# A hand-planned attention block on one core: the planner's transfer queue, the last output tile of block 2, and the first key evacuation

## The chip, the core and the metric

The kernel runs on one core of one Trainium2 chip. The metric is device microseconds (us) of one execution. Before the change the median of three runs is 410.35 us (410.2 to 410.64). Names used below: PE is TensorE (matmul), ACT is ScalarE, DVE is VectorE, POOL is GpSimd, SP is SyncE, which here only issues transfers (DMAs).

## The reference, cut to what matters

```python
# x (1, 2048, 448), wqkv (448, 1344), wo (448, 448), all bf16; 16 heads of 28
qkv = (x @ wqkv).reshape(B, S, 3, H, Dh).transpose(2, 0, 3, 1, 4)
q, k, v = qkv[0], qkv[1], qkv[2]
scores = einsum("bhqd,bhkd->bhqk", q, k) * Dh ** -0.5
p = softmax(scores, axis=-1)
o = einsum("bhqk,bhkd->bhqd", p, v)
out = o.transpose(0, 2, 1, 3).reshape(B, S, D) @ wo
```

## The kernel before, in words

**Tiles.** The 16 heads are four groups (g) of four heads, each head padded from 28 to 32 rows; the 2048 queries are four blocks (c) of 512. A window is one group and one query block; there are 16. In a window, every key tile of 128 keys (16 of them) gives four score tiles, one for each head, of 128 keys by 512 queries: 1024 score tiles in all. A score tile is one matmul (line 854) of a key tile (KB) and a query tile (QB). Both hold 64 rows for a head: 32 of the head and 32 that carry a bound on the scores, so that the exponent never overflows; the bound's rows are filled by transfers (KB<-NK at lines 591 and 613, QB<-QP at line 706).

**Exponentials on two routes.** Most score tiles go in pairs through ACT: two matmuls fill the two banks of PA0 or PA1, one activation (line 1277) of 128x1024 writes PTA. The others go through one bank of PD and a polynomial: three DVE passes (lines 1058, 1061, 1077) and one POOL product (line 1064), or one DVE copy (line 990) and six POOL passes (lines 997 to 1020). They write PTD. The value product (line 1122) then takes the four exponentials of a key tile into PO; a column of ones in VA sums the denominators.

**The planner.** The order of every engine's instructions is not written down. The function builds a list of `Op`s with an estimated duration, a latency, dependencies and a priority, runs a small event loop over them (lines 1313 to 1375) with one clock for PE, ACT, POOL, DVE and SP, and then issues the instructions in the order of the planned start times (lines 1380 to 1392). At run time each engine takes its own instructions strictly in that order and waits on semaphores where data is missing. Which route a score tile takes is also decided there, by which buffer is free at the planned time. So a changed constant can move any instruction behind it.

**Normalizing a window.** When a window's last value product is done, DVE copies PO to OSB (line 942). SP fetches the sums (line 949), DVE inverts them (line 951), SP stores them to DRAM (line 952) and reads them back as a broadcast over 128 partitions, 256 KB (line 954, RRB), for which the planner counts a latency of GLAT = 6.5. POOL multiplies (line 957) and leaves OT for the output projection. The same SP queue carries the query transfers of the next windows: two copies (line 700) and four bound rows (line 706), each planned with QLAT = 2.6.

**Key bounds.** For groups 1 to 3, `task_kmax` makes the largest key per row (line 571), then NK on DVE (line 615), then four broadcast transfers (line 613). For group 0 the first 512 keys do not go over transfers: their score columns in PD0 are evacuated by ACT, twice, to KB0_0 and KB0_1 (line 538).

**Start.** The input is loaded, transposed on PE (line 414), evacuated (lines 425, 427), projected to keys (line 522) and queries (line 652); DVE writes the bound rows of the first two query tiles itself (line 678).

**End.** In the last group, `task_OP` makes the output of a query block from its four OT tiles, four 128-row tiles (tq) for each block: matmuls at line 804, then a DVE evacuation. For blocks 2 and 3 the first three groups were summed earlier (`SPLIT`, `task_part`), so that only the last group is missing and DVE adds the two (line 808). One transfer stores a block (line 817). The last block is done by hand behind the plan (lines 1393 to 1408): DVE transposes PO (line 866), inverts the sums (867), transposes them back in halves (870), multiplies (1399); PE projects (1401); ACT or DVE evacuates (1407, 1405); four transfers store (1408). The first three groups' share for tiles 0, 1 and 3 is put into PD banks by nine matmuls (line 888, `late_sums`).

Of the kernel before, what the change touches and what calls it, by code (L numbers as in the profile page):

```python
# [9 lines left out]
ACT = mybir.ActivationFunctionType  # L10
ALU = mybir.AluOpType
# [7 lines left out]
P = 128  # L19
H = 16  # L20
HP = 32
G = 4
HG = 4
CC = 4
QW = 512
# [57 lines left out]
def kernel(  # L83
# [7 lines left out]
    nc = tc.nc  # L91
    _, S, D = x.shape
    Dh = D // H
    CK = D // CC
    NQC = S // QW
    NKT = S // P
    TPC = QW // P
# [41 lines left out]
    QEA = 20  # L139
    PLT = 6.0  # L140
    GLAT = 6.5
    J3 = 9
    UQ = 60
    OD = 2
# [6 lines left out]
    LOOK = 0.2  # L151
    SLK = 0.13
    MG = 0.1
    SPLIT = {2: (0, 1, 2, 3), 3: (2,)}
    ACCQ = (0, 1, 3)
    ACCP = 2000
    PARTD = 60
# [19 lines left out]
    KP0 = -4395  # L177
    KP1 = -4000
    VE = 16
    UV = 4  # L180
    BW = (-1, 2, 0)
    THF = (0, 1, 0, 0)
    EVP = (-1200, -4365, -700, 0)
    KEVP = (0, 200, 200, 200)
# [134 lines left out]
    log = []  # L319
# [9 lines left out]
    def add(op):  # L329
        static[op.eng].append(op)  # L330
        return op

    def bank_task():
        return {"slot": None}
# [173 lines left out]
    def task_K(g, sc):  # L508
# [19 lines left out]
        if g == 0:  # L528
# [8 lines left out]
            if sc == 0:  # L537
                evs = [add(Op("ACT", 0.67, lambda pr=pr: nc.scalar.activation(
                    out=KB[0][pr][:, cs], in_=ap(), func=ACT.Identity, bias=bndcol[pr][:, 0:1], scale=selcol[pr][:, 0:1]),
                    deps=[ops[-1], redmm], prio=KP0 if pr == 0 else KP1, lat=0.17)) if pr == 0 or KENG[0] == "ACT" else  # L540
                    add(Op("DVE", EVK, lambda pr=pr: nc.vector.tensor_scalar(
                        out=KB[0][pr][:, cs], in0=ap(), scalar1=selcol[pr][:, 0:1], scalar2=bndcol[pr][:, 0:1], op0=ALU.mult, op1=ALU.add),
                        deps=[ops[-1]], prio=-4360)) for pr in range(2)]
                for i in range(HG):
                    kev[(g, sc, i)] = evs[i // 2]
            else:
                evs = [add(Op("ACT", 0.62, lambda: nc.scalar.activation(
                    out=KB[1][0][:, cs], in_=ap(), func=ACT.Identity, bias=onescol[:, 0:1], scale=1.0),
                    deps=[ops[-1]], prio=prio + KEVP[sc], lat=0.17) if KENG[sc] == "ACT" else Op("DVE", EVK, lambda: nc.vector.tensor_scalar(  # L549
                        out=KB[1][0][:, cs], in0=ap(), scalar1=onescol[:, 0:1], scalar2=None, op0=ALU.add),  # L550
                        deps=[ops[-1]], prio=prio + 0.1 + KEVP[sc]))]
                k0ev[sc] = evs[0]
                evs[0].acq = lambda t: red.start is None or red.done(t)
                red.acq = lambda t: evs[0].start is None or evs[0].done(t)
# [12 lines left out]
    def task_kmax(g):  # L567
# [42 lines left out]
        def rep_out(i, c0):  # L610
# [1 line left out]
            n = (S - c0 * QW) // P  # L612
            nc.sync.dma_start(out=KB[g % 2][i // 2][HP * st:HP * (st + 1), c0 * QW:S].rearrange("p (r q) -> p r q", q=P),
                              in_=NK[g][HP * SI[i]:HP * (SI[i] + 1), None, :].to_broadcast([HP, n, P]))
        nk = add(Op("DVE", 0.2, lambda: nc.vector.tensor_scalar(
            out=NK[g][:], in0=maskm[:, 0:P], scalar1=KMAX[g][:, 0:1], scalar2=None, op0=ALU.mult), deps=[m], prio=prio + 0.2, elig=elig))
        for i in (2, 3, 0, 1):
            o = add(Op("SP", DISS + 0.07, (lambda i=i: rep_out(i, c0)), deps=[nk] + ([deps[i]] if i < 2 else []),
                       prio=due + 0.3 + 0.001 * i, lat=DLAT + 0.6))
# [176 lines left out]
    def task_OP(c):  # L796
        due = (12 + c + 1) * WT + 16
        st = add(Op("SP", 0.05, None, prio=due))
        evs = []
        for tq in range(TPC):  # L800
            task = bank_task()
            ap = (lambda task=task: bank(task)[:, 0:D])
            g0 = G - 1 if c in SPLIT else 0
# [9 lines left out]
            def aft(t, task=task):  # L813
                task["slot"].free_at = t + SEM
            ev.after = aft
            evs.append(ev)
        add(Op("SP", 0.05, lambda: nc.sync.dma_start(out=out_perm[:, c * TPC:(c + 1) * TPC, :], in_=OUTS[c][:]),
               deps=evs, prio=due))

    SEGS = [(FB * w, FB * (w + 1)) for w in range(NF)] + [(FB * NF + (NKT - FB) * w, FB * NF + (NKT - FB) * (w + 1)) for w in range(NF)]  # L820

# [494 lines left out]
    times = [0.0]  # L1316
    port = [0.0]
    lock = [0.0]
    seen = set()
    ends = []  # L1320
    seq = 0
    while True:
# [12 lines left out]
        while progress:  # L1335
            progress = False
            for e in ("ACT", "PE", "POOL", "DVE", "SP"):
# [27 lines left out]
                    heapq.heappush(times, t + o.dur + PGAP)  # L1365
                o.start = t
                o.end = t + o.dur
                free[e] = o.end
                log.append((t, seq, o))
                seq += 1  # L1370
# [9 lines left out]
    log.sort(key=lambda e: (e[0], e[1]))  # L1380
    sync = mybir.DependencyInfo(mybir.DependencyClass.Sync, mybir.DependencyReason.DATA)
    issued = []
    for _, _, o in log:
        if o.fn is None:
            continue
        r = o.fn()
        if o.eng == "DVE" and r is not None:
            issued.append((o, r))
        elif o.eng == "POOL" and o.kind in ("p", "n", "g"):
            before = [d for d in issued[-8:] if d[0].end <= o.start + 1e-6 and (d[0].kind == "sb" or d[0].end <= o.start - PLD + 1e-6)]  # L1390
            if before:
                tc.add_manual_dep(r.ins, before[-1][1].ins.name, sync)
    c = NQC - 1
    g = G - 1
    hw = QW // 2
    fb = {tq: PD[late_acc[tq]][:, 0:D] if tq in late_acc else PA[1 - acts[-1][2].idx][:, 0:D] for tq in range(TPC)}

    def half_out(hf):
        nc.vector.tensor_tensor(out=OTL[hf], in0=PO[:, hf * hw:(hf + 1) * hw], in1=DEN[hf], op=ALU.mult)
        for tq in (2 * hf, 2 * hf + 1):  # L1400
            nc.tensor.matmul(out=fb[tq], lhsT=OTL[hf][:, (tq % 2) * P:(tq % 2 + 1) * P], rhs=WO[:, g, :], start=(tq not in late_acc), stop=True)
    norm_dve(PO[:], DT[:], DR[:], lambda hf: DEN[hf], half_out)
    for tq in range(TPC):
        if tq in SPLIT[c]:
# [31 lines left out]
```

## Time and profile before

| what | us |
|---|---|
| median of three runs | 410.35 |
| span of the profiled execution, first to last instruction | 408.4 |
| median less that span | 1.95 |
| ACT busy, share of the span | 394.3 (97%) |
| DVE busy | 382.0 (94%) |
| PE busy | 359.9 (88%) |
| POOL busy | 329.2 (81%) |
| last exponential ends (timeline of ACT) | 399.2 |

The profiled execution has no other time of its own than its span; the 1.95 us are what the runs' median has beyond it. The profile has a page (shares, a strip of 40 slices, the costliest groups) and answers questions of the trace: a timeline of one engine, the chain of work that ended last, who waited for whom. A timeline row gives the start, the length, the engine, the line, the operation, the tiles, the shape and how many equal instructions were merged in it; in brackets stands the idle time ahead of it and what ended that. Two ACT instructions that follow each other overlap in it: the next one starts before the last has written all of its output, so the distance between ends is what an exponential costs.

### The profile page before, as it was taken

What the parts mean: (1) busy time and instruction counts of PE and PEld (TensorE: products, weight loads), DVE (VectorE), ACT (ScalarE), POOL (GpSimd) and SP (SyncE); (2) the same over time, 40 slices, a digit from 0 to 9 for tenths busy, and PEclk for the clock granted to TensorE, in tenths of its full rate; (3) what the DMA queues carried; (4) which work ended last, traced back from release to release, by engine and by line L of the source; (5) the groups of instructions that cost most, each with busy time, mean ns of one, the idle gap of its engine ahead of it and who ended that gap; (6) DMA issues with size and microseconds to landing.
All of it is one profiled execution on the core that took longest, in us unless ns stands there. A gap on an engine that the chain in (4) does not pass through costs nothing.

```text
span 408.4 us, 7572 instructions
## 1 busy us (share of the span) xinstructions
PE 359.9 (88%) x2599; PEld 120.2 (29%) x2599; DVE 382.0 (94%) x673; ACT 394.3 (97%) x433; POOL 329.2 (81%) x352
## 2 busy tenths in 40 slices
PE   8999989798898989889898989888898988889994
PEld 5243232223233232322323232232322222223231
DVE  6996999999999999999999999999999999999985
ACT  4999999999999999999999999999999999999992
POOL 4048999778699889978697987999679988999870
PEclk9999999999999999999999999999999999999998
DMA  9251130101501020110501000010230001010112
GB/s 220 44 86 43 42 76 2 29 30 39 108 1 34 13 40 0 24 52 6 104 2 46 2 20 29 8 41 2 64 80 3 28 4 43 2 35 13 49 72 90
DMA packets 36302, 16.58 MB, mean 41 GB/s; under 512 B 28768, under 2 KB 32992, under 8 KB 36264
## 3 DMA queue, kind: packets, MB, share of 16 engines
q1 hardware_dynamic: 35656, 15.89, 16.5%
q8 instruction: 20, 0.33, 0.3%
q10 hardware_dynamic: 608, 0.22, 0.2%
q14 instruction: 18, 0.15, 0.1%
HBM read 7.44 MB, written 1.97 MB: 23 GB/s over the span
## 4 chain that ended last, share of the span: by engine, by line
ACT 55%; PE 25%; DVE 11%; issue 7%; DMA 1%; DVEq 0%; ACTq 0%
ACT PTA L1277 54%; PE PA L854 9%; PE PO L1122 7%; PE PD L854 3%; DVE DU L1058 2%; DVE DV L1061 2%; DVE PTD L1077 1%; DMA QB<-QP 1%; PE PO L652 1%; PE PA L393 1%; DVE QB L678 1%; PE PO L1238 1%; DVE QB L662 1%; DVE KB L549 1%; DVE KB L557 1%
## 5 line engine op out<-in xcount | busy, mean ns | idle before, releaser
L1277 ACT ACTIVATE PTA<-PA 128x1024 bf16<-128x1024 f32 x422 | 387.3, 1183 | 0.4 <-PE PA L854 0.2
L1064 POOL TENSOR_TENSOR DG<-DV,DU 128x512 f16<-128x512 f16 x157 | 179.9, 1156 | 49.5 <-DVE DV L1061 40.4
L854 PE MATMUL PA<-QB,KB 64*128 64x512 bf16 x843 | 168.3, 380 | 38.3 <-ACT PTA L1277 35.6
L854 PEld LDWEIGHTS <-KB 64*128 64x128 bf16 x1024 | 66.2, 93 | 180.7 <-issue 173.4
L1058 DVE TENSOR_SCALAR DU<-PD 128x512 f16<-128x512 uint16 x157 | 104.3, 680 | 7.2 <-PE PD L854 6.7
L1077 DVE SCALAR_TENSOR_TENSOR PTD<-PD,DG 128x512 uint16<-128x512 f32 x157 | 105.6, 680 | 3.1 <-POOL DG L1064 2.2
L1061 DVE SCALAR_TENSOR_TENSOR DV<-PD,DU 128x512 f16<-128x512 uint16 x157 | 104.5, 678 | 0.6
L1122 PE MATMUL PO<-PTA,VA 128*32 128x512 bf16 x843 | 86.4, 386 | 0.6 <-DVE QB L662 0.4
L854 PE MATMUL PD<-QB,KB 64*128 64x512 bf16 x181 | 65.6, 377 | 1.8 <-DVE PTD L1077 0.9
L1122 PE MATMUL PO<-PTD,VA 128*32 128x512 bf16 x181 | 52.9, 386 | 0.0
L1122 PEld LDWEIGHTS <-VA 128*32 128x32 bf16 x1024 | 19.7, 94 | 50.4 <-issue 49.7
L1003 POOL TENSOR_TENSOR GV<-GE,GU 128x512 f16<-128x512 f32 x24 | 27.8, 1159 | 2.5 <-DVE QP L691 0.8
L1005 POOL TENSOR_TENSOR GU<-GV,GU 128x512 f16<-128x512 f16 x24 | 27.8, 1156 | 1.5 <-DVE QP L691 0.8
L1007 POOL TENSOR_TENSOR SG<-SG,GU 128x512 f32<-128x512 f32 x24 | 27.8, 1157 | 1.2 <-DVE QP L691 0.6
L997 POOL TENSOR_SCALAR GU<-SG 128x512 f16<-128x512 uint16 x24 | 14.9, 619 | 7.5 <-DVE SG L990 4.7
L990 DVE COPY SG<-PD 128x512 f32<-128x512 f32 x24 | 16.4, 681 | 4.0 <-PE PD L854 3.8
L957 POOL TENSOR_TENSOR OT<-OSB,RRB 128x512 bf16<-128x512 f32 x15 | 19.1, 1273 | 0.4 <-DVE QP L691 0.4
L652 PE MATMUL PO<-XT,WQP 112*128 112x512 bf16 x56 | 18.7, 386 | 0.4 <-DVE KB L549 0.4
L1020 POOL TENSOR_SCALAR PTD<-SG 128x512 uint16<-128x512 f32 x24 | 14.9, 620 | 3.0 <-DVE QP L691 1.9
L1000 POOL TENSOR_SCALAR GE<-SG 128x512 f32<-128x512 uint16 x24 | 14.9, 619 | 1.9
L723 PEld LDWEIGHTS <-XT 112*128 112x128 bf16 x256 | 13.4, 98 | 9.4 <-issue 9.2
L522 PE MATMUL PO<-XT,WKP 112*128 112x512 bf16 x48 | 15.9, 386 | 0.0
(105 smaller groups left out, 194.2 us busy)
## 6 DMA issues: line engine op xcount, KB each, us to landing
RRB<-SCR SPq DMA_DIRECT2D x15, 256.0 KB
QB<-QP SPq DMA_DIRECT2D x56, 32.0 KB
KB<-NK SPq DMA_DIRECT2D x12, 128.0 KB
XS<-in_x_dram SPq DMA_DIRECT2D x3, 448.0 KB
out_dram<-XS SPq DMA_DIRECT2D x3, 448.0 KB
QB<-QB SPq DMA_DIRECT2D x28, 32.0 KB
KB<-KB SPq DMA_DIRECT2D x6, 128.0 KB
RRB<-SCRF SPq DMA_DIRECT2D x2, 256.0 KB
```

Of the source, the lines that this page charges most:

```text
L652: ops = chain_mm(CC, lambda cc: nc.tensor.matmul(out=ap(), lhsT=WQP[g][:, cc, :], rhs=XT[c][cc // 2][0:CK, cc % 2, :], start=(cc == 0), st ...
L854: nc.tensor.matmul(out=ap, lhsT=KB[g % 2][i // 2][a:a + 64, j * P:(j + 1) * P], rhs=QB[w % NQB][i // 2][a:a + 64, :], start=True, stop=Tru ...
L957: o5 = add(Op("POOL", 1.22, lambda: nc.gpsimd.tensor_tensor(out=OT[g][c][:], in0=OSB[b][:], in1=RRB[b][:], op=ALU.mult), deps=o4, prio=-10 ...
L1003: g3 = add(Op("POOL", PTT, lambda: nc.gpsimd.tensor_tensor(out=GV[:], in0=GE[:], in1=GU[:], op=ALU.mult), deps=[g2], prio=prio + 2, kind=" ...
L1005: g4 = add(Op("POOL", PTT, lambda: nc.gpsimd.tensor_tensor(out=GU[:], in0=GV[:], in1=GU[:], op=ALU.mult), deps=[g3], prio=prio + 3, kind=" ...
L1007: g5 = add(Op("POOL", PST, lambda: nc.gpsimd.tensor_tensor(out=X[:], in0=X[:], in1=GU[:], op=ALU.add), deps=[g4], prio=prio + 4, kind="g", ...
L1058: p1 = add(Op("DVE", P1, lambda: nc.vector.tensor_scalar(out=DU[b][:], in0=lo, scalar1=SIG / 65536, scalar2=SIG * (SS - 0.5), op0=ALU.mult ...
L1061: p2 = add(Op("DVE", P1, lambda: nc.vector.scalar_tensor_tensor(out=DV[b][:], in0=lo, scalar=65536 * (SS - 0.5 + CE / C3), in1=DU[b][:], o ...
L1064: gq = add(Op("POOL", PTT, lambda: nc.gpsimd.tensor_tensor(out=DG[b][:], in0=DV[b][:], in1=DU[b][:], op=ALU.mult), deps=[p2], prio=n, kind ...
L1077: f = add(Op("DVE", P1, lambda: nc.vector.scalar_tensor_tensor(out=PTD[st["s"].idx][:].bitcast(U16), in0=PX[slot.idx][:], scalar=EBITS + C ...
L1122: nc.tensor.matmul(out=PO[HP * st:HP * (st + 1), :], lhsT=VA[g][:, j, st, :], rhs=r["p"][i][1](), start=first, stop=last, tile_position=(0 ...
L1277: nc.scalar.activation(out=PTA[pslot.idx][:, 0:len(ns) * QW], in_=PA[s.idx][:, 0:len(ns) * QW], func=ACT.Exp, bias=ACT_BIAS, scale=ACT_SCALE)
```

## The change

It has four parts, all in the one function.

1. **Planner.** When SP issues a broadcast with latency GLAT, the planner notes the time until which the queue is taken (RNGB = 6.2 behind the issue). A transfer that SP issues before that time is planned to land not before it, each 0.35 (RNGN) behind the last. This alters planned latencies, so the order of instructions; it adds no instruction.
2. **Last output tile of block 2.** Tile 3 of block 2 leaves `SPLIT` and `task_OP`. `late_tile` makes it right behind the last value product in the issue order: four matmuls (all four groups) into the free half of a PA buffer, a copy on ACT, a transfer of 112 KB of its own. The other three tiles are stored by one transfer of 336 KB. The three `late_sums` matmuls of tile 3 of block 3 are held back and issued behind the first half of the last projection.
3. **First key evacuation.** KB0_0 of group 0's first 512 keys is evacuated by DVE (`tensor_scalar`) and no longer by ACT; KB0_1 stays on ACT and is planned behind it.
4. **Smaller ones.** NK of groups 1 to 3 moves from DVE to POOL; BW, which tells after which of the first window's four bound rows a transposed input is evacuated, goes from 2 to 4 for input block 1.

```diff
+    RNGB = 6.2
+    RNGN = 0.35
...
-    SPLIT = {2: (0, 1, 2, 3), 3: (2,)}
+    SPLIT = {2: (0, 1, 2), 3: (2,)}
+    ATQ = 3
...
-    BW = (-1, 2, 0)
+    BW = (-1, 4, 0)
...
                 evs = [add(Op("ACT", 0.67, lambda pr=pr: nc.scalar.activation(
                     out=KB[0][pr][:, cs], in_=ap(), func=ACT.Identity, bias=bndcol[pr][:, 0:1], scale=selcol[pr][:, 0:1]),
-                    deps=[ops[-1], redmm], prio=KP0 if pr == 0 else KP1, lat=0.17)) if pr == 0 or KENG[0] == "ACT" else
+                    deps=[ops[-1], redmm], prio=KP1, lat=0.17)) if pr else
                     add(Op("DVE", EVK, lambda pr=pr: nc.vector.tensor_scalar(
                         out=KB[0][pr][:, cs], in0=ap(), scalar1=selcol[pr][:, 0:1], scalar2=bndcol[pr][:, 0:1], op0=ALU.mult, op1=ALU.add),
-                        deps=[ops[-1]], prio=-4360)) for pr in range(2)]
+                        deps=[ops[-1], redmm], prio=KP0)) for pr in range(2)]
+                evs[1].deps.append(evs[0])
...
-        nk = add(Op("DVE", 0.2, lambda: nc.vector.tensor_scalar(
-            out=NK[g][:], in0=maskm[:, 0:P], scalar1=KMAX[g][:, 0:1], scalar2=None, op0=ALU.mult), deps=[m], prio=prio + 0.2, elig=elig))
+        nk = add(Op("POOL", 0.25, lambda: nc.gpsimd.tensor_scalar(
+            out=NK[g][:], in0=maskm[:, 0:P], scalar1=KMAX[g][:, 0:1], scalar2=0.0, op0=ALU.mult, op1=ALU.add), deps=[m], prio=prio + 0.2, elig=elig))
...
         for tq in range(TPC):
+            if c == NQC - 2 and tq == ATQ:
+                continue
...
-        add(Op("SP", 0.05, lambda: nc.sync.dma_start(out=out_perm[:, c * TPC:(c + 1) * TPC, :], in_=OUTS[c][:]),
+        n = len(evs)
+        add(Op("SP", 0.05, lambda: nc.sync.dma_start(out=out_perm[:, c * TPC:c * TPC + n, :], in_=OUTS[c][:, 0:n, :]),
                deps=evs, prio=due))
+
+    def late_tile(ap):
+        c, tq = NQC - 2, ATQ
+        for g in range(G):
+            nc.tensor.matmul(out=ap, lhsT=OT[g][c][:, tq * P:(tq + 1) * P], rhs=WO[:, g, :], start=(g == 0), stop=(g == G - 1))
+        nc.scalar.copy(out=OUTS[c][:, tq, :], in_=ap)
+        nc.sync.dma_start(out=out_perm[:, c * TPC + tq:c * TPC + tq + 1, :], in_=OUTS[c][:, tq:tq + 1, :])
...
+    ring = [0.0]
...
+                if e == "SP" and o.fn is not None and pos[0] > 0:
+                    if o.lat == GLAT:
+                        ring[0] = t + RNGB
+                    elif t < ring[0]:
+                        ring[0] += RNGN
+                        o.lat = max(o.lat, ring[0] - o.end)
...
+    last_v = [o for _, _, o in log if o.kind == "V"][-1]
+    spare = PA[1 - acts[-1][2].idx]
+    held = []
     for _, _, o in log:
         if o.fn is None:
             continue
+        if o.kind == "A" and o.prio >= ACCP + ACCQ[-1]:
+            held.append(o)
+            continue
         r = o.fn()
+        if o is last_v:
+            late_tile(spare[:, QW:QW + D])
...
         for tq in (2 * hf, 2 * hf + 1):
             nc.tensor.matmul(out=fb[tq], lhsT=OTL[hf][:, (tq % 2) * P:(tq % 2 + 1) * P], rhs=WO[:, g, :], start=(tq not in late_acc), stop=True)
+        for o in held if hf == 0 else ():
+            o.fn()
```

More of the change, by code (lines that the diff above doesn't have):

```diff
@@ L1395 @@
     hw = QW // 2
-    fb = {tq: PD[late_acc[tq]][:, 0:D] if tq in late_acc else PA[1 - acts[-1][2].idx][:, 0:D] for tq in range(TPC)}
+    fb = {tq: PD[late_acc[tq]][:, 0:D] if tq in late_acc else spare[:, 0:D] for tq in range(TPC)}
     def half_out(hf):
```

## The prediction

> **What bounds the kernel now.** I read the strip of 40 slices first. ACT is full in all slices but the first and the last, so the time is a start, a stream of exponentials on ACT, and an end. Then the timeline of ACT:
>
> ```profile
> 9.08 0.77 ACT L538 ACTIVATE KB<-PD,bndcol,selcol 128x512 bf16<-128x512 f32 x1
> ...
> 11.31 23.48 ACT L1277 ACTIVATE PTA<-PA 128x1024 bf16<-128x1024 f32 x25
> 34.52 0.77 ACT L916 ACTIVATE RR<-PD 128x512 f32<-128x512 f32 x1
> 35.00 142.45 ACT L1277 ACTIVATE PTA<-PA 128x1024 bf16<-128x1024 f32 x155
> 177.68 221.54 ACT L1277 ACTIVATE PTA<-PA 128x1024 bf16<-128x1024 f32 x242 [0.23 <-PE PA L854]
> 403.74 1.53 ACT L1407 CAST XT<-PD 128x448 bf16<-128x448 f32 x3 [4.53 <-PE PD L1401]
> ```
>
> Distances between ends tell what a step costs. L916 ends at 35.29, the 155 exponentials behind it at 177.45: 142.16 / 155 = 0.917 each. A half one (128x512) costs 34.52 + 0.77 - 34.79 = 0.50. Of the 422 exponentials the last is a half one (the list by form has one of 128x512, 0.70 long). The last row: alone at 177.68 an exponential is 1.02 long, ends at 178.70; (399.22 - 178.70 - 0.50) / 240 = 0.917 again, so nothing is lost there. Lost is: in the break 178.70 - 177.45 - 0.92 = 0.33; in the first row, whose first ends at 12.34, 34.79 - 12.34 - 24 x 0.917 = 0.44. No more than 0.77 of 388 us can be had by a smoother stream; the rest is the number of exponentials, the start and the end.
>
> The end, in the timelines of PE and DVE:
>
> ```profile
> 399.52 0.39 PE L1122 MATMUL PO<-PTA,VA 128*32 128x512 bf16 x4
> 399.84 0.74 PE L888 MATMUL PD<-WO,OT 128*128 128x448 bf16 x3
> 400.42 0.35 PE L804 MATMUL PD<-WO,OT 128*128 128x448 bf16 x1
> 400.61 1.61 PE L888 MATMUL PD<-WO,OT 128*128 128x448 bf16 x6
> 403.34 0.55 PE L1401 MATMUL PD<-WO,QB 128*128 128x448 bf16 x2 [1.13 <-DVE QB L1399]
> ```
> ```profile
> 398.87 1.15 DVE L808 TENSOR_TENSOR XS<-PD,KB 128x448 bf16<-128x448 f32 x2
> 400.81 0.62 DVE L808 TENSOR_TENSOR XS<-PD,KB 128x448 bf16<-128x448 f32 x1 [0.79 <-PE PD L804]
> 401.35 0.71 DVE L866 STREAM_TRANSPOSE SG<-PO 128x512 f32<-128x512 f32 x1
> ```
>
> PO is complete at 399.91, but DVE first waits for the fourth output tile of block 2 (L804 at 400.42) and transposes PO at 401.35. ACT meanwhile is idle for 4.53.
>
> **The change, part by part.** Orders of the changed kernel are those of its built instructions; durations are rows of before.
>
> *Late tile, about -1.35.* The fourth L808 leaves DVE. The third ends at 398.87 + 1.15 = 400.02, PO at 399.91: the transpose can start at 400.0, not 401.35. In the new order two L808 again stand behind the last L1077, so DVE's queue ahead of the transpose is as before less one. If DVE runs ahead, PO bounds: 0.06 behind the last exponential's end (399.21) plus 0.39, so -1.65; if L1077 comes 0.65 later than before, -0.7.
>
> *What it adds, about +0.2.* PE gets four late matmuls behind the last value product, then five L888: nine against ten before (399.84 to 402.22, 0.24 each), so 2.15; L1401 is due 1.99 behind the transpose, which starts 0.1 behind PO. That just fits. Three L888 are held between the halves of L1401: 3 x 0.19 (0.55 less 0.36, a step at L1401) to 3 x 0.24. PE was free there from 403.72 to 404.15, 0.43; the second half comes 0.13 to 0.3 later. ACT's copy (0.53, as L1407) lies in 4.53 of idle time. SP issues two stores, each about 0.34, some 2 us ahead of the first L1408; were they late, the last stores would be as late. End: -1.15.
>
> *Head, about -0.45.* Before, ACT does L538 twice (ends 0.67 and 0.68 apart) and its first exponential waits for that. Now DVE evacuates KB0_0 (0.75, as L549 and L662, the same shape from PSUM): behind L534 (8.73) to 9.48, then L672 and L674 (0.21 a step) to 9.97, then the four bound rows L678 (0.36 each): 10.37, 10.73, 11.09, 11.45. The second row was ready at 10.47 before, so DVE's chain is 0.26 later; but the first pair of score matmuls now ends at 10.73 + 0.06 + 0.38 = 11.17 and its exponential starts at 11.23 instead of 11.31. The second pair ends at 11.89, so the second exponential goes on without a gap. Before it had to wait for the third and fourth rows, behind a 0.69 copy on DVE, and started 1.13 behind the first (12.44). Gained by then: 0.08 + 0.21. Two smaller gaps follow before, in the timeline at 14.35 (0.07) and 20.94 (0.18, where PE waited 0.42 for L549 to free PO; in the new order value products, not L652, come next in PO). All together -0.55 at best. Against it: DVE's copies and QB1 follow about 0.8 later, and with them NK (20.07 before), and SP now issues one more KB copy (0.6) ahead of the four first broadcasts: last one issued at about 23.9, not 22.86. Two exponentials that need them come at 26; landing takes about 2 us, by the traffic. Slack falls from about 1.7 to near 0. I take +0.1 for it; bounds 0 and 0.5.
>
> *One half exponential less: -0.50.* The new order has 421 double ones and no half one; DVE takes one score tile more, 3 x 0.68 = 2.04, and the evacuation, 0.75. It gives up three NK (L615 is 0.70 each, 2.1) and one L808 (0.62): +0.07 of 382, hidden, as DVE isn't the stream's bound. If it were not hidden it would show as exponentials that wait for PTD's value products, 0.07.
>
> *NK on POOL: 0.* Shapes near it on POOL: 0.20 (L457, 128x16) and 0.62 (L1020, 128x512); three of them in 75 us of idle time. What waits behind it is below.
>
> *Queue order, about -0.33.* The break at 177.68 is the only one of its kind:
>
> ```profile
> 171.78 0.58 SPq L954 DMA_DIRECT2D RRB<-SCR  x1
> 172.47 2.43 SPq L706 DMA_DIRECT2D QB<-QP  x4
> ```
> ```profile
> 176.97 0.11 PEld L854 LDWEIGHTS <-KB 64*128 64x128 bf16 x3 [0.89 <-DMA QB<-QP]
> ```
>
> The broadcast is issued 0.69 ahead of the query rows, and the first score matmul that needs them waits until 176.97, 4.5 behind their issue (planned 3.2). Rows of the same size that SP issued at 178.72 with nothing ahead of them had moved their packets 1.5 later. So the wait is real, and in the new order no score tile needs a query row issued within 5 exponentials behind a broadcast. Bounds -0.33 and 0, since nothing else waits so. The Trainium skill speaks against the model: "DMA: Bandwidth & Descriptors", section "Queues, rings and completion order", says that each engine takes a ring's descriptors in order, but that completion is not first in, first out for an issuing engine. By that rule a transfer may pass the broadcast and this term would be 0; by the row it did not pass, and the row decides.
>
> *New breaks, +0.3.* From the first score tiles on, the order is another on every engine. Before has one break of 0.33 in 400 steps; a new order can bring as many, or more: bounds 0 and 1.0.
>
> **Sum.** -1.35 + 0.2 - 0.45 - 0.5 - 0.33 + 0.3 = -2.13. Span 408.4 to 406.3; with the 1.95 that the median has beyond the span, 408.2.
>
> **Rivals.**
> 1. *The end gives its gain back.* DVE, 94% busy and with one tile more, ends its last L1077 late, or the held L888 run at the 0.27 of the row at 400.61 (1.61 / 6) and push the second half. For it: DVE's L1077 ended only 0.25 ahead of the last exponential. Against: one operation less in front. The end brings -0.3 instead of -1.15: 409.1.
> 2. *The planner's change does nothing, or the new order fits worse.* One break alone depended on it; without it 408.5. If the new order loses what seven such breaks would (2.0 in place of 0.3 and the 0.33), little is left: 410.2. Against: the old order lost only 0.77 in all.
> 3. *Slower: NK on POOL holds up SP.* POOL takes its instructions in order; NK stands behind a DG (1.16), a GU or a DG in the three groups, and SP, in order too, holds the four broadcasts and all behind them until it is done. PE already waited 0.2 for KB<-NK once (at 198.91), so there is hardly slack. A DG that itself waits for DVE (POOL idles 40 us on that in all) makes each of three groups up to 1.16 late, 3.5 in sum: 411.7. It decides from 0.7 of loss per group, where the gain of 2.13 is used up. Against: in the new order KMAX stands six to nine exponentials ahead of the first use, 5.5 to 8 us.
>
> **How the numbers follow.** About 0.2% (0.8 us) is what a measurement of this kernel can tell from no change. Forecast 408.2: 0.64. Rival 1: 0.16. Rival 2: 0.13, mostly in "same". Rival 3: 0.07. Faster takes the forecast and nearly all of rival 1, and a little of rival 2: 0.82; same 0.11; slower 0.07. The forecast's own bounds: end -1.5 to -0.4, head -0.55 to -0.05, break -0.33 to 0, new breaks 0 to 1.0, the half one fixed. All best together is 407.5; the runs of before lie up to 0.3 from their median, so 407.2. To hold rival 1 and the bad side of the new breaks I go up to 409.7, which leaves out most of rivals 2 and 3.
>
> **What would show it.** Right: the timeline of ACT has 421 exponentials with ends 0.917 apart, the first starting near 11.2, and no break by QB<-QP; L866 starts 0.6 to 0.9 behind the last exponential's end (2.14 before); from L866 to the end of the span 0.2 more than the 7.05 of before. Wrong: ACT idle for "PE PA L854" in more than two places, PE waits for KB<-NK near 26, or near 100, 200 and 300, L866 behind a late L808 or L1077, or PE still in L888 when the second L1399 is done.

## The result, and the profile after

The changed kernel takes **408.52 us** (median of 4 runs, 408.49 to 408.62); the kernel before took 410.32 beside it (4 runs, 410.2 to 410.64). The ratio is 0.9956, 95% interval 0.9942 to 0.997. The forecast was 408.2 with a range of 407.2 to 409.7. The profiled execution has a span of 406.7 (408.4 before).

The timeline of ACT for the kernel after, to be read against the one shown of before:

```profile
9.86 0.79 ACT L541 ACTIVATE KB<-PD,bndcol,selcol 128x512 bf16<-128x512 f32 x1
11.02 13.86 ACT L1291 ACTIVATE PTA<-PA 128x1024 bf16<-128x1024 f32 x15 [0.37 <-PE PA L868]
25.44 1.02 ACT L1291 ACTIVATE PTA<-PA 128x1024 bf16<-128x1024 f32 x1 [0.56 <-PE PA L868]
26.94 9.27 ACT L1291 ACTIVATE PTA<-PA 128x1024 bf16<-128x1024 f32 x10 [0.47 <-PE PA L868]
...
36.46 362.45 ACT L1291 ACTIVATE PTA<-PA 128x1024 bf16<-128x1024 f32 x395
```

The first exponential starts at 11.02 (11.31 before). L541 stands once, where L538 stood twice. The break at 177.68 is gone: the 395 exponentials from 36.46 to 398.91 are 0.917 apart but for 0.13 us in all. All 421 are double ones. But there are two breaks that before did not have, ahead of the 16th and the 17th exponential: in ends, 26.46 is 0.67 and 27.96 is 0.58 later than the step of 0.917 would make them.

The end, in the timelines of DVE and of PE for the kernel after:

```profile
398.40 1.15 DVE L814 TENSOR_TENSOR XS<-PD,KB 128x448 bf16<-128x448 f32 x2
399.60 0.72 DVE L880 STREAM_TRANSPOSE SG<-PO 128x512 f32<-128x512 f32 x1
```
```profile
398.85 0.36 PE L902 MATMUL PD<-WO,OT 128*128 128x448 bf16 x1
399.14 0.40 PE L1136 MATMUL PO<-PTA,VA 128*32 128x512 bf16 x4
399.47 0.93 PE L830 MATMUL PA<-WO,OT 128*128 128x448 bf16 x4
400.24 1.11 PE L902 MATMUL PD<-WO,OT 128*128 128x448 bf16 x5
401.60 0.55 PE L1430 MATMUL PD<-WO,QB 128*128 128x448 bf16 x2 [0.24 <-DVE QB L1428]
```

The transpose (L880) starts 0.69 behind the last exponential's end (2.14 before). It is 0.05 behind both the L814 ahead of it (399.55) and the last value product, which completes PO (399.54). Six of the nine L902 stand ahead of the first L1430, three between its halves. From the transpose to the end of the span it is 7.10 (7.05 before).

Summed up by the prediction's steps (losses in ends of exponentials, which add up to the span):

| step | forecast | measured |
|---|---|---|
| last exponential's end to the transpose, 2.14 to 0.69 | -1.35 | -1.45 |
| transpose to the end, 7.05 to 7.10 | +0.2 | +0.05 |
| first exponential's end, 12.353 to 12.045 | -0.08 | -0.31 |
| three small gaps of the head (0.20, 0.07, 0.18) gone | -0.47 | -0.45 |
| key bounds late: the two breaks | +0.1 | **+1.25** |
| one half exponential less | -0.50 | -0.50 |
| break behind the broadcast | -0.33 | -0.33 |
| other breaks, 0.05 to 0.13 | +0.3 | +0.08 |
| sum | -2.13 | -1.66 (span: -1.7) |

0.12 of the 0.31 are there ahead of any part that was changed (the first reduction on DVE starts at 7.73 and not 7.85).

### The profile page after: what moved, and what is told of

Read it like the earlier page. It is cut to its first block, busy times and chain, and to the rows that moved or that the text cites. A ratio compares the mean times of both kernels' runs of the same rounds, so it can differ in the third digit from the quotient of the medians.

```text
span 406.7 us, 7592 instructions
## 1 busy us (share of the span) xinstructions
PE 361.3 (89%) x2606; PEld 120.6 (30%) x2606; DVE 382.5 (94%) x672; ACT 393.5 (97%) x432; POOL 330.9 (81%) x356
## 3 DMA queue, kind: packets, MB, share of 16 engines
HBM read 7.44 MB, written 1.97 MB: 23 GB/s over the span
## 4 chain that ended last, share of the span: by engine, by line
ACT 74%; PE 14%; issue 7%; DVE 3%; POOL 0%; POOLq 0%; ACTq 0%
ACT PTA L1291 74%; PE PA L868 6%; PE PO L1136 4%; PE PD L868 2%; PE PD L810 1%; PE PO L810 1%; DVE DU L1072 0%; DVE DV L1075 0%; PE PO L525 0%; DVE WKP L381 0%; PE PD L525 0%; PE PD L902 0%; PE PO L1252 0%; DVE WO L318 0%; PE PD L1430 0%
## 5 line engine op out<-in xcount | busy, mean ns | idle before, releaser
L868 PE MATMUL PA<-QB,KB 64*128 64x512 bf16 x842 | 167.4, 380 | 38.3 <-ACT PTA L1291 35.5
L868 PEld LDWEIGHTS <-KB 64*128 64x128 bf16 x1024 | 67.6, 93 | 182.0 <-issue 173.8
L1091 DVE SCALAR_TENSOR_TENSOR PTD<-PD,DG 128x512 uint16<-128x512 f32 x158 | 106.9, 682 | 3.6 <-POOL DG L1078 2.7
L1075 DVE SCALAR_TENSOR_TENSOR DV<-PD,DU 128x512 f16<-128x512 uint16 x158 | 105.9, 683 | 1.0
L868 PE MATMUL PD<-QB,KB 64*128 64x512 bf16 x182 | 65.2, 377 | 0.6
L656 PE MATMUL PO<-XT,WQP 112*128 112x512 bf16 x56 | 18.7, 386 | 0.0
L525 PE MATMUL PO<-XT,WKP 112*128 112x512 bf16 x52 | 16.9, 385 | 0.0
```

The lines of the kernel that those rows point to most:

```text
L656: ops = chain_mm(CC, lambda cc: nc.tensor.matmul(out=ap(), lhsT=WQP[g][:, cc, :], rhs=XT[c][cc // 2][0:CK, cc % 2, :], start=(cc == 0), st ...
L868: nc.tensor.matmul(out=ap, lhsT=KB[g % 2][i // 2][a:a + 64, j * P:(j + 1) * P], rhs=QB[w % NQB][i // 2][a:a + 64, :], start=True, stop=Tru ...
L1075: p2 = add(Op("DVE", P1, lambda: nc.vector.scalar_tensor_tensor(out=DV[b][:], in0=lo, scalar=65536 * (SS - 0.5 + CE / C3), in1=DU[b][:], o ...
L1091: f = add(Op("DVE", P1, lambda: nc.vector.scalar_tensor_tensor(out=PTD[st["s"].idx][:].bitcast(U16), in0=PX[slot.idx][:], scalar=EBITS + C ...
```

## Where the two breaks come from

Ahead of the breaks, in the timeline of PE for the kernel after (L868 into PA is the pair of score matmuls of one exponential):

```profile
23.75 0.76 PE L727 MATMUL PD<-WV,XT 112*128 112x112 bf16 x12
24.44 0.61 PE L1136 MATMUL PO<-PTA,VA 128*32 128x512 bf16 x8
24.99 0.41 PE L868 MATMUL PA<-QB,KB 64*128 64x512 bf16 x2
25.39 0.55 PE L727 MATMUL PD<-WV,XT 112*128 112x112 bf16 x8
25.98 0.59 PE L656 MATMUL PO<-XT,WQP 112*128 112x512 bf16 x2
26.51 0.60 PE L868 MATMUL PA<-QB,KB 64*128 64x512 bf16 x4
```

PE is idle for no more than 0.05 here (ahead of the first L656, which waits for DVE's copy of PO), and no row waits for a transfer. The 16th pair stands behind 24 other matmuls (the 20 of the first two rows and four at 23.42). It starts 0.11 behind the end of the 15th exponential (24.88), whose PA buffer the plan gives it. The 17th stands behind ten others. By the kernel's code the planner counts a pair as ready only when its bounds have landed, and these pairs are the first that need the broadcast bounds (L595); so it put other work there. In the timelines of SP, of the kernel before and of the kernel after:

```profile
20.82 2.68 SPq L591 DMA_DIRECT2D KB<-NK  x4
```
```profile
18.32 3.21 SPq L585 DMA_DIRECT2D KB<-KB  x5
21.63 2.67 SPq L595 DMA_DIRECT2D KB<-NK  x4
```

The bounds go out 0.81 later, NK on DVE (L580) 0.84 later, and the exponentials that need them come 0.76 sooner. Of the 0.84, 0.78 are not DVE's work but a wait. The evacuation of the second queries in the DVE timeline, before and after:

```profile
13.30 0.75 DVE L662 TENSOR_SCALAR QB<-PD,offscol 128x512 bf16<-128x512 f32 x1
```
```profile
14.01 0.75 DVE L666 TENSOR_SCALAR QB<-PD,offscol 128x512 bf16<-128x512 f32 x1 [0.78 <-PE PD L656]
```

With BW at 4 the copy of input block 1 (L428) comes behind all four bound rows, at 11.35 and not 10.50; PE, which needs it for the second queries (L656), is that much later, and DVE is idle 0.78 for them.

## The experiments

The kernel before was run beside every batch: 410.44, 410.38, 410.34 and 410.28. Ratios are to it. In e1, e5, e6, e8, e9, e11, e12 and e13 the order of all other instructions stays; e2, e3, e4 and e10 are planned anew, so that their order is another from some point on. In the diffs, `put(a, b)` issues a ahead of b, `s15` and `s[15]` are the score pair of the 16th exponential (the lists count from 0), and `x[k]` the exponentials.

### The transfer queue: e1, e2, e10

**e1**, the kernel before; one broadcast (L954, issued at 171.78) goes behind the four query rows that stood behind it:

```diff
+    sp = [e[2] for e in log if e[2].eng == "SP" and e[2].fn is not None]
+    for k, o in enumerate(sp):
+        if o.lat == GLAT and k + 4 < len(sp) and all(x.lat == QLAT and abs(x.prio - sp[k + 1].prio) < 0.5 for x in sp[k + 1:k + 5]) and pos_at[id(o)] > 400:
+            put(o, sp[k + 5])
+            break
```

> The kernel before with one thing moved: on SP the broadcast of 256 KB that was issued at 171.78 goes behind the four query rows that followed it (issued from 172.47). Theory 'queue order': the rows landed 4.5 after their issue because the broadcast was ahead of them; now they land about 2 after it, PE's wait of 0.89 for QB<-QP near 177 goes, and the break of 0.33 with it: span 408.4 to 408.1 (time 410.3 to 410.0). Rival 'late anyway': rows and score tiles are late for another reason (DVE's passes, the number of transfers in flight); the wait stays at 0.5 or more and the time at 410.3.

Measured: 409.78, ratio 0.9979 (0.9961 to 0.9998), span 408.1. The break at 177.68 is gone from ACT's timeline, and the wait of 176.97 from PE's (the rows are issued at 171.91). A new one of 0.12 stands at 104.2. The break was made by the broadcast ahead of the rows, and is worth about 0.3 by the spans (the medians differ by 0.66, which the trace doesn't account for). The DMA packets in the two traces show how. Before, 24 of the 32 packets of each row move about 1.2 behind the row's issue, and the last 8 of each only from 175.9 to 176.6, when the broadcast's packets (173.15 to 176.19) are nearly through. In e1 all 32 of each row move about 1.2 behind its issue.

**e2**, the kernel before with the queue model alone:

```diff
+    RNGB = 6.2
+    RNGN = 0.35
...
+    ring = [0.0]
...
+                if e == "SP" and o.fn is not None and pos[0] > 0:
+                    if o.lat == GLAT:
+                        ring[0] = t + RNGB
+                    elif t < ring[0]:
+                        ring[0] += RNGN
+                        o.lat = max(o.lat, ring[0] - o.end)
```

> The kernel before with the planner's queue model alone (the order is planned anew; it has 421 double exponentials and no half one, which is 0.50 less on ACT). Theory 'it does what it says': no PE wait for QB<-QP, so 0.33 less besides, and no new break over 0.3: time 409.5. Rival 'too cautious': the model plans key bounds and rows behind a broadcast later than they land, PE is given other work ahead of score pairs that could run, and ACT shows new breaks of 0.5 to 1.1 where a key group begins (near 100, 200 or 300): time 410.3 or more.

Measured: 411.93, ratio 1.0023 (1.0006 to 1.0041; runs 410.7 to 412.62), span 409.1. The profiled execution is one of the quicker ones (410.91), so about 1.0 of the median is not in the trace. No wait for a transfer is left, and no half exponential, but the new order has breaks of 0.58 at 113.0 and of 0.20, 0.33 and 0.66 between 299 and 305: between 301.5 and 303.3 PE does 28 value products ahead of one score pair. The rival's time came; that the model's caution made these breaks, as the rival says, is not shown. What the model takes away is smaller than what a new plan can bring.

**e10**, the kernel after without the queue model:

```diff
                     if o.lat == GLAT:
-                        ring[0] = t + RNGB
+                        ring[0] = t
```

> The changed kernel without the planner's queue model (part 1 taken out, planned anew; the other parts stay). The start is the same up to about 55 us, with its two breaks. Theory 'queue order': without the model at least one score tile is put shortly behind query rows or key bounds that SP issued behind a broadcast, and PE waits there for the transfer: a break of 0.3 to 0.8 by QB<-QP or KB<-NK, 408.8 to 409.4. Rival 'the model does nothing': no wait for such a transfer, 408.3 to 408.7, and what differs is one half exponential more or less (0.5) or the length of the end.

Measured: 410.46, ratio 0.9998 (0.9982 to 1.0015), span 408.6. Both ranges miss. The rival has the mechanism (no such wait, another end), but not the size. PE waits for no transfer (one weight load waits 0.42 for QB<-QP at 278.97, and no exponential is late by it), and the last exponential ends at 399.18, only 0.26 later than in the kernel after. The rest, 1.64, is in the end. Its DVE timeline:

```profile
400.99 0.63 DVE L814 TENSOR_TENSOR XS<-PD,KB 128x448 bf16<-128x448 f32 x1 [0.97 <-PE PD L810]
401.53 0.70 DVE L880 STREAM_TRANSPOSE SG<-PO 128x512 f32<-128x512 f32 x1
```

In this order the third L810 stands behind the four late matmuls of L830 on PE (at 400.60), and the transpose behind its L814: 401.53, later even than the 401.35 before the change. The model's part in the gain of the whole is thus the order it happened to lead to, and not a wait for a transfer that this plan would otherwise have had.

### The end: e3, e8, e12

**e3**, the kernel before with the late tile and the held sums alone (all of part 2 of the change):

```diff
-    SPLIT = {2: (0, 1, 2, 3), 3: (2,)}
+    SPLIT = {2: (0, 1, 2), 3: (2,)}
...
+        if o is last_v:
+            late_tile(spare[:, QW:QW + D])
```

> The kernel before with the late output tile alone (planned anew: 422 double exponentials, 0.43 more on ACT than 421 and a half one). Theory: the end, from the last exponential's end to the end of the span, falls from 9.19 to 7.8 as in the changed kernel; the stream up to there stays as before but for the 0.43; time 410.3 - 1.4 + 0.43 = 409.35. Rival: the late tile's end gained only in company of a DVE that runs ahead; end above 8.5 and time at 410 or more.

Measured: 410.21, ratio 0.9992 (0.9977 to 1.0008), span 408.4. Two of its rows, from the timelines of PE and of DVE:

```profile
177.36 0.39 PE L865 MATMUL PD<-QB,KB 64*128 64x512 bf16 x1 [1.03 <-DMA QB<-QP]
```
```profile
401.27 0.72 DVE L877 STREAM_TRANSPOSE SG<-PO 128x512 f32<-128x512 f32 x1 [1.36 <-PE PO L1133]
```

The last exponential ends at 400.01, 0.80 later than before: the half one has become a whole one (0.43), and the break behind the broadcast has grown to 0.77 (0.33 before). And DVE is done with its output tiles at 399.91, but PO is not there: PE turns to a pile of about 40 value products only at 398.88, so that the transpose is 1.26 behind the stream and not 0.69. The end is 8.4 long, near the rival's 8.5, and the time is the rival's. The late tile takes DVE's wait away; PO must be ready for that to count.

**e8**, the kernel after; the late tile is copied by DVE:

```diff
-        nc.scalar.copy(out=OUTS[c][:, tq, :], in_=ap)
+        nc.vector.tensor_copy(out=OUTS[c][:, tq, :], in_=ap)
```

> The changed kernel, but the late tile's copy is made by DVE, where it stands ahead of the transpose of PO; matmuls and stores stay. Theory: what the old end lost was DVE waiting for the last output tile. The late matmuls end at 400.40, the copy takes 0.62, so the transpose starts near 401.0 instead of 399.60 and the span grows by 1.4 to 408.1 (time 409.9). Rival: the end is set by PE (matmuls held back) or by the stores, then the span grows by 0.5 or less.

Measured: 410.63, ratio 1.0004 (0.9992 to 1.0017), span 408.9. Its DVE timeline:

```profile
400.90 0.63 DVE L831 CAST XS<-PA 128x448 bf16<-128x448 f32 x1 [1.33 <-PE PA L830]
401.45 0.71 DVE L880 STREAM_TRANSPOSE SG<-PO 128x512 f32<-128x512 f32 x1
```

The theory holds, with a larger price than its 1.4: the transpose is 1.85 later than in the kernel after, 0.55 for the copy and 1.3 for its wait for PE. The other 0.3 of the 2.2 stand behind the transpose, where PE's clock is halved (last section): from the transpose to the end it is 7.42 here, and 7.08 in e10, whose clock stays full. So the whole gain of the end hangs on the transpose not standing behind the late tile.

**e12**, the kernel after with the sums not held back:

```diff
-        if o.kind == "A" and o.prio >= ACCP + ACCQ[-1]:
-            held.append(o)
-            continue
```

> The changed kernel with the three late sums (L902) of the last block's tile 3 no longer held back: all nine stand ahead of the first L1430, the rest is the same order. Theory (the end's working in the prediction): thirteen matmuls behind the last value product fill PE until about 402.0, so the first half of L1430 starts about 0.35 later (401.6 to 402.0), the second about 0.15 earlier; ACT's three casts follow each other and the end is 0.2 to 0.3 later: 408.7 to 408.8. Rival: the held matmuls between the halves are themselves what the end waits for, and without them it is 0.15 earlier: 408.35.

Measured: 408.56, ratio 0.9954 (0.9938 to 0.997), span 406.7. Both miss: it makes no difference. The first half of L1430 starts at 401.74 (0.14 later), the second at 402.39 (0.16 earlier); the last store on ACT's queue is issued 0.13 earlier, the last on SP's ends 0.07 later.

### The head: e4, e9

**e4**, the kernel before with KB0_0 evacuated by DVE and BW at 4 (part 3 and half of part 4):

```diff
-    BW = (-1, 2, 0)
+    BW = (-1, 4, 0)
...
-                    deps=[ops[-1], redmm], prio=KP0 if pr == 0 else KP1, lat=0.17)) if pr == 0 or KENG[0] == "ACT" else
+                    deps=[ops[-1], redmm], prio=KP1, lat=0.17)) if pr else
...
+                evs[1].deps.append(evs[0])
```

> The kernel before with the first key evacuation on DVE and BW = 4 alone (planned anew: 422 double exponentials, +0.43). Theory 'the head costs': start 0.3 earlier, the three early gaps (0.45) gone, but breaks of 1.25 at the 16th and 17th exponential: +0.5, and with 0.43 the time is 411.2. Rival 'the breaks came with another part': no breaks at 25 to 27, time 410.3 - 0.75 + 0.43 = 410.0.

Measured: 412.76, ratio 1.0048 (1.0027 to 1.0069; runs 410.61 to 413.77), span 411.4. The breaks of the kernel after are there, at the same two exponentials (1.59 and 1.50 between ends), so they belong to this part, and neither to the queue model nor to the late tile. Of the rest, 1.1 is a late input in the profiled execution (PE waits for XS), and 2.6 are four breaks at 207 to 213, part of them at half clock (last section), which begin with this row of PE:

```profile
206.35 0.39 PE L855 MATMUL PD<-QB,KB 64*128 64x512 bf16 x1 [1.97 <-DMA KB<-NK]
```

The list of SP's waits tells why: the four bounds of group 2 (L614) wait 3.8 for the key copies L604, which were issued at 197.75 and 198.38 behind a broadcast of 196.51. The queue model is missing in this kernel. Its end is short without a late tile: DVE has all four output tiles behind it at 403.93, and the transpose is 0.51 behind the last exponential. So an order alone can do what part 2 does.

**e9**, the kernel after in its own order, KB0_0 evacuated by ACT:

```diff
-                    add(Op("DVE", EVK, lambda pr=pr: nc.vector.tensor_scalar(
-                        out=KB[0][pr][:, cs], in0=ap(), scalar1=selcol[pr][:, 0:1], scalar2=bndcol[pr][:, 0:1], op0=ALU.mult, op1=ALU.add),
+                    add(Op("DVE", EVK, lambda pr=pr: nc.scalar.activation(
+                        out=KB[0][pr][:, cs], in_=ap(), func=ACT.Identity, bias=bndcol[pr][:, 0:1], scale=selcol[pr][:, 0:1]),
```

> The changed kernel, but KB0_0 of the first 512 keys is evacuated by ACT at the same place of the order; the order of everything else is kept. ACT's chain ahead of the first exponential is longer by 0.68, it starts near 11.3 instead of 11.02. Theory 'taken up': the exponentials up to the 15th run into the breaks at 25 and 27, which are set by other things, so a later start only makes those breaks smaller: span 406.5 to 406.8 (time 408.3 to 408.6), the two breaks about 0.3 smaller in sum. Rival 'the start counts': the breaks keep their size and the span grows by 0.3 to 407.0 (time 408.8).

Measured: 408.66, ratio 0.9951 (0.9932 to 0.9969), span 406.9. The first exponential starts 0.2 later and everything follows; the two breaks keep their size (0.67 and 0.59), as the rival said. NK is at 20.91 as in the kernel after, although DVE has 0.80 less to do, and L666 waits 0.85 for PE in place of 0.78. In this order the evacuation on DVE is worth about 0.2 by the spans and does not make the bounds late.

### The two breaks: e5, e6, e11, e13

**e5**, the kernel after; the pairs of the 16th and the 17th exponential go ahead on PE:

```diff
+    put(s15, later(s14, "PE", "W"))
+    vs = [o for o in (later(s15, "PE", "V", n) for n in range(2))]
+    put(s16, later(vs[1], "PE", "W"))
```

> The changed kernel with one thing moved: the score pairs of the 16th and the 17th exponential stand on PE ahead of the value matmuls and products, and of the projection, that stood ahead of them. The changed kernel loses 0.67 and 0.58 at these two exponentials (ends 1.59 and 1.50 apart in place of 0.917), 1.25 in sum. Theory 'order': PE is busy with that other work because the plan took the key bounds (KB<-NK) to land later than they do; the two breaks shrink to 0.6 or less in sum, the span goes from 406.7 to about 406.0 (time 407.8). Theory 'data': the bounds land just then; PE now waits for them instead, a wait of PE for KB<-NK of some 0.6 or more shows, breaks and span stay (406.7, time 408.5).

Measured: 409.28, ratio 0.9968 (0.9956 to 0.9981), span 407.5: slower than the kernel after. One row of PE's timeline and one of ACT's (up to 28 us):

```profile
24.78 0.39 PE L868 MATMUL PA<-QB,KB 64*128 64x512 bf16 x1 [0.26 <-DMA KB<-NK]
```
```profile
25.20 2.85 ACT L1291 ACTIVATE PTA<-PA 128x1024 bf16<-128x1024 f32 x3 [1.21 <-PE PA L868]
```

Now PE does wait for the bounds: it goes on at 24.13, which is 2.47 behind the issue of the first (21.66), and at 24.78, 2.40 behind that of the second (22.38). But the experiment has a flaw of mine. The 15th and 16th exponential use the same buffer, and the moved pair comes in the program ahead of the exponential that was still to read it. So the 15th exponential waits for the 16th's scores, and is taken from them: part of the computation is changed, and the 1.21 is that wait. What the run shows is when the bounds land, 2.4 behind their issue, and no more.

**e6**, as e5, with the four broadcasts ahead of the fifth key copy on SP (first at 21.27) and the 17th pair one piece of work earlier:

```diff
+    put(cps[0], nxt[0])
...
-    put(s16, later(vs[1], "PE", "W"))
+    put(s16, vs[0])
```

> As e5, and SP issues the four key-bound broadcasts ahead of the one KB copy of 32x1024 that had come ahead of them (it ran 0.6, NK was done 0.4 ahead of the first broadcast's issue); the second pair stands one step earlier on PE. Theory 'order': with both, the breaks go below 0.2 in sum; span about 405.5 (time 407.3). Theory 'data': the broadcasts land 0.4 earlier, so the two breaks lose about 0.4 of their 1.25; span 406.3 (time 408.1). If the KB copy had nothing to do with it, e6 equals e5.

Measured: 409.63, ratio 0.9974 (0.9959 to 0.9989), span 407.8. It has the same flaw (15th exponential), and breaks of 0.93, 0.95 and 0.36.

**e11**, the kernel after; NK of group 0 ahead of L553 on DVE, the broadcasts ahead of the fifth key copy, and eight pairs ahead on PE:

```diff
+    put(nk[0], ev3[0])
+    put(cps[0], nxt[0])
...
+    put(s[15], later(s[14], "PE", "W", 1))
+    put(s[16], later(s[15], "PE", "V"))
+    put(s[17], later(s[16], "PE", "W"))
...
+    put(s[22], later(s[21], "PE", "V", 2))
```

> The changed kernel with three moves in its issue order and nothing else: on DVE the key bounds' NK of group 0 (L580) goes ahead of the last key evacuation (L553), on SP the four first broadcasts of it (L595) go ahead of the fifth key copy (L585), and on PE the pairs of score matmuls of the 16th to 23rd exponential each go one to three pieces of other work ahead. Theory 'late bounds': the two breaks at 26.5 and 28.0 us (0.67 + 0.58 in ends) are there because the bounds arrive 0.8 later than before the change, and moving the scores ahead without them only put PE behind a transfer. With the first broadcast issued at about 20.9 (21.63 in the changed kernel), its second is there at about 24.0, the fourth at about 25.4, and the breaks shrink to 0.1 to 0.3: 1.0 to 1.1 us less than the changed kernel, 407.4. Rival 'PE is full': PE's work in the first 32 us is what bounds, so pairs moved ahead give the time back as later breaks, as in the two runs that moved only the scores: 408.4 or more, with new breaks between 28 and 32 or near 47.

Measured: 410.33, ratio 0.9996 (0.998 to 1.0012), span 408.5. The same flaw, six times over (the 16th to 21st exponential are taken from the pair two later): the 16th starts at 27.25, 2.26 idle. It tells nothing of PE's load. It does show that NK can be at 20.49 and the broadcasts at 21.06.

**e13** repairs this. From the 16th exponential on the two buffers are swapped, and each pair stands behind the exponential that reads its buffer:

```diff
+    put(nk[0], ev3[0])
+    put(cps[0], nxt[0])
...
+    for k, n in enumerate((2, 5, 6, 8, 10, 12, 14, 16, 18, 20, 22, 23, 25, 26, 29, 31, 33, 36, 38), 15):
+        if at_log(s[k]) > at_log(rest[n]):
+            put(s[k], rest[n])
+        if at_log(x[k - 2]) > at_log(s[k]):
+            put(x[k - 2], s[k])
...
+    for k in range(15, len(s)):
+        other_bank(s[k], s[k].fn)
+        other_bank(x[k], x[k].fn)
```

> The changed kernel with its issue order altered at the two breaks: from the 16th exponential on, the two PA buffers are swapped, so that the 15th and the 16th no longer use the same one; NK of group 0 (L580) goes ahead of the last key evacuation on DVE and the four first broadcasts (L595) ahead of the fifth key copy on SP; and the score pairs of the 16th to 34th exponential go up to four pieces of other work ahead on PE, each still behind the exponential that reads its buffer. All data are those of the changed kernel. Theory 'same buffer and late bounds': in the changed kernel the 16th pair starts 0.11 behind the end of the 15th exponential because it needs its buffer, and the 17th is behind other work; with the other buffer the 16th pair can start at about 24.1, the 17th is held by the fourth broadcast until about 25.4, and the 1.25 of the two breaks shrink to 0.3 to 0.5: 407.6 to 407.9. Rival 'PE is full': what PE has to do by 32 us leaves no room, the time comes back as breaks between 28 and 40 us of 0.7 or more, and the time is 408.2 or more.

Measured: 410.06, ratio 0.9995 (0.9986 to 1.0005), span 408.3. Its timeline of ACT:

```profile
11.05 23.27 ACT L1291 ACTIVATE PTA<-PA 128x1024 bf16<-128x1024 f32 x25 [0.37 <-PE PA L868]
34.59 1.94 ACT L1291 ACTIVATE PTA<-PA 128x1024 bf16<-128x1024 f32 x2 [0.28 <-PE PA L868]
...
42.56 2.85 ACT L1291 ACTIVATE PTA<-PA 128x1024 bf16<-128x1024 f32 x3 [0.58 <-PE PA L868]
46.44 354.05 ACT L1291 ACTIVATE PTA<-PA 128x1024 bf16<-128x1024 f32 x386 [1.03 <-PE PA L868]
```

At the spot the theory holds: the first 25 exponentials lose 0.25 in place of 1.25, all at the 17th, whose pair takes 0.65 on PE and not 0.39 (25.27 to 25.92; by e5's 2.4 the fourth bound, issued at 23.0, is there at 25.4). So early bounds and the other buffer together take 1.0 of the 1.25 away. But the time comes back, and 1.6 more: breaks of 0.38, 0.39, 0.68 and 1.13 up to 47.5. PE's row there:

```profile
45.40 0.61 PE L1136 MATMUL PO<-PTA,VA 128*32 128x512 bf16 x6 [1.23 <-DVE KB L561]
```

The value products that now come behind the scores free PO later, so DVE copies it (L939) at 26.30 and not 25.25; POOL's products (DG) are at 38.77 and not 37.11; DVE's key evacuation (L561) that frees PO for the value products at 45.40 is at 44.61 and not 42.54. The rival named PE as what is full; these rows point to the chain PE, DVE, POOL and back, which in this order has no slack in the first 48 us. Its time, 408.2 or more, is what came.

No version beat the changed kernel: e12 is equal to it (408.56), e9 0.14 behind, within the measurement.

## Why the prediction was right, and where it was not

1. **Late tile**, -1.35: right, -1.45. The working had the output tile's addition ahead of the transpose as what bounds it, 0.1 behind PO. In the kernel after it is PO: where PO was ready early (before, e8, e10), the transpose starts 0.08 ahead of the end of the DVE instruction in front of it; here it starts 0.05 behind PO, as in e3, where DVE sat idle for PO (complete at 401.22, transpose at 401.27). PO itself is later than the working's bound for it (-1.65): the last value products start 0.23 behind the last exponential, with an L902 in front, and not 0.06. e8 shows the price of the alternative, e3 and e10 that the order in front decides (PO late, an L810 late).
2. **What it adds**, +0.2: 0.05. The half of L1430 that is held up is later by 0.16 (e12 against the kernel after), near the 0.13 to 0.3 of the working, but it is not what the end waits for alone: without it the first half is later by 0.14.
3. **Head**, -0.45: wrong, a net +0.49 (-0.31 - 0.45 + 1.25). The failing step is "Slack falls from about 1.7 to near 0. I take +0.1 for it; bounds 0 and 0.5." The mechanism, bounds late for the two exponentials that need them first, was named; the sum was mis-sized. That NK comes about 0.8 later was forecast too, but from DVE's added work. The last of DVE's copies ends no later than before (13.24, 13.27 before), and e9, without that work, has NK as late: what delays it, by the trace, is DVE's wait for the second queries, which came with BW at 4. Its 26 for the exponentials that need them was an old date: at 0.917 a step, the 17th is due at 11.02 + 16 x 0.917 = 25.7. And "landing takes about 2 us" was 2.4 from the issue to the matmul (e5), so the fourth, issued at 23.67, is there at 26.1, and its exponential can start 0.4 later, at 26.5. Slack was -0.8, not 0, by this estimate. The remaining 0.45 is put down to the plan, which gave the 16th pair the buffer of the 15th and set other work ahead of the 17th; e13 takes both away together, so the split is worked out and not measured. The working had also looked for the loss as a wait of PE for KB<-NK; it came as PE doing other work, which no list of PE's waits shows.
4. **Half exponential**, -0.50: right, and read from the built order alone.
5. **NK on POOL**, 0: right. It takes 0.37 there, and PE never waits for KB<-NK near 100, 200 or 300; rival 3 did not come. It has no run of its own.
6. **Queue order**, -0.33: right for this kernel, and e1 shows the cause. The Trainium skill's rule that completion is not first in, first out ("DMA: Bandwidth & Descriptors", "Queues, rings and completion order") did not make it 0: in three kernels (before, e3, e4) transfers behind a broadcast were there 4.5 to 5.1 us after their issue. The rule and the wait go together: three quarters of a row's packets did pass the broadcast (e1's section), and the first score matmul still waited until 176.97, behind the last of them. But the model is not what the break's absence hangs on: e10 has no model and no such wait. It was absent in both orders planned with the model (e2, after), and present in three of four without, in two of these (before, e3) at the same place.
7. **New breaks**, +0.3: 0.08 outside the head. e2, e4 and e13 show that the bound of 1.0 was too narrow for another order: 1.8, 2.6, 2.6.

That the forecast came within 0.3 of the time is in part luck, because the errors partly cancelled: +1.15 at the bounds, -0.25 at the end, -0.2 at the start (0.12 of it ahead of any changed part), -0.2 in new breaks. The parts do not add up: alone, the model, the end and the head come to +1.5, -0.2 and +2.3 by their medians, together to -1.8. Each of these was planned anew, so each has the luck of its own order in it, and e4 a halved clock in most of its runs as well.

What stays open: whether BW alone, without DVE's evacuation in the plan, brings the two breaks (the trace says so, no run of its own), and whether a plan made anew with the bounds early would keep the gain of e13's first 25 exponentials.

## What to carry to other kernels

When a stream is made to start sooner, date anew every transfer that it needs: step length times number from the new start, against issue plus measured landing. A break where the feeding engine is busy shows in no list of that engine's waits; read that engine's order. And an edit to a hand-planned kernel is worth what its order makes of it: read the built order, and price edits with the rest of the order held fixed.

## What the runs showed of the hardware

**PE's clock can fall after 2 us of waiting.** In e4 PE waited 1.97 us up to 206.35. The windows of that run (span, PE, PEld, DVE, ACT and POOL busy, then PE's granted clock as the third number from the end):

```profile
207.00:207.80 0.80, 0.80 (x11) 0.11 (x3) 0.00 (x0) 0.75 (x1) 0.80 (x1) 1.00 0.45 110
208.00:211.00 3.00, 3.00 (x21) 0.55 (x20) 2.48 (x4) 2.22 (x4) 1.49 (x2) 0.50 0.17 44
```

It runs at full clock for 1.5 us, then at half for about 3.4 (to 211.3; a pair of scores takes 0.61 and not 0.39), and three more exponentials lose 1.2. Of e4's twelve runs the quickest (410.61) is the only one with a mean granted clock of 1.000; the others have 0.989 to 0.996 and 411.85 to 413.77. In e8 the same: 2.06 of waiting up to 403.44, half clock from 404.3, the last L1430 0.58 long and not 0.35. In e10 a wait of 2.00 was followed by no such fall in the 1.5 us that PE still worked. The Trainium skill ("TensorE: Matmul & The Clock Gate", "HAM oscillation — how this bites in real kernels") says that no idle gap over about 3.4 us is to be left; here two gaps of 2 us were followed by half clock and a third was not. What decides between them is not shown.

**A short DVE operation can wait for POOL.** NK on DVE (128x128, bf16) took 0.24 in e2 and e4 where POOL did nothing, and 0.70 (three times in before, once in e2), 0.55 (e2) and 0.83 (e4) where a TENSOR_TENSOR was running on POOL; each of these six ended 0.05 behind POOL's instruction. The 0.70 that the prediction counted for it was mostly this wait.
